# TensorE transposes by 64-row halves, and softmax sums divided out on the rows of x, in a fused attention and mixture-of-experts kernel

## The chip, the cores and the metric

The kernel runs on one core of one Trainium2 chip. The metric is the device time of one execution in microseconds (us). Three runs of the kernel before gave a median of 738.96 us (736.74 to 739.04).

## The reference

The three stages are chained. All arithmetic is float32.

```python
# attention: q, k, v are [4 batches, 8 heads, 576 rows, 64]; a band mask of 64 keys
scores = (1 / sqrt(64)) * q @ k.T                 # kept where 0 <= row - key < 64
attn = exp(scores - max); attn /= attn.sum() + 1e-9
x = (attn @ v) as [2304 rows, 8 heads * 64]
# mixture of experts, top 1 of 8, 512 -> 1024 -> 512
logits = x @ w_gate + modality_bias[modality_id]
e = argmax(logits); gate = softmax(logits)[e]
x = gate * (relu(x @ w1[e]) @ w2[e])
# feed-forward, 512 -> 2048 -> 512
h = x @ w_in
out = (h - tanh(h)) @ w_out
```

## The kernel before, in words

**Attention.** A batch has five groups: four head pairs (`t_pair`) of 512 rows, and one tail (`t_tail`) with the last 64 rows of all heads. `t_prep` turns the k and then the q of a pair with four TensorE transposes of 128x128 each (L611, L619), each into one PSUM bank; DVE copies k out (`t_kcopy`, L638), ACT or DVE copies q out (L628, L630). A pair then has four TensorE bursts: scores of both heads (L709, L722), transposes of the probabilities P in 16 halves of 64 rows that go to two banks (L747), and P times v (L761). Between scores and transposes stands `t_soft`, once per head: DVE takes the row maxima (L790), ACT the exponentials and their sums (L793), DVE adds 1e-9 to the sums and inverts them (L796, L797), and POOL or DVE multiplies P by the result (L799). `t_xout` copies the product to xT, which holds x with the channels on the partitions.

**Routing** (`route`, once per batch). L901 multiplies xT by the gate weights, 32 columns per head pair; `t_logit` copies the partial logits out; L918 turns them and sums over the four head pairs by a product with a 0/1 matrix `sel`. DVE then finds the expert and the gate value, and the place of each row in its expert's list. `t_xrow` turns a tile of 128 rows of x with four full transposes (L873) into one bank, one ACT or DVE instruction multiplies by the gate (L879, L881), and SP sends the tile to DRAM (L884): five tiles a batch, 20 in all.

**Experts.** Five units hold the rows of one expert each: four of 504 rows (four blocks of 126) and one of 288 (126, 126 and 36). Two of them are formed early, from batch 0 and from batches 0 to 2. `t_gather` fetches the rows of a unit from DRAM, `t_xsplit` turns them with full transposes (L1306), one bank for each of four column blocks, and `t_xsplit1` (L1316, L1319) makes a high and a low part. `t_stream` runs the two matrix products (L1381, L1401) as three products of high and low parts. `t_wload` and `t_wsplit` (L392, L394, L1356) bring and split the weights. `t_conv` decodes the 64-bit weights of the feed-forward in the background.

**Feed-forward** (`second`): L1788 and L1836, in six chunks of 384 rows.

**Order of the work.** Everything up to the feed-forward is ordered before the launch by a planner, `Flow`: each task yields operations with an engine (or a choice of engines with a price each), the tasks it waits for, the PSUM banks it may take (`bank`, `nb` of them) and a priority. `Flow.pick` takes the engine that could start first and, of the operations ready on it, the one with the lowest priority number. A pseudo-random `nudge` from one SEED is added to the priorities from 0 to 30 on all engines but SP. The engines then run their queues in that order and wait only on semaphores. Attention may use banks 0 to 3, 6 and 7 (`bankA`), routing and x banks 4 and 5 (`bankX`), the experts' products 6 and 7 (`bankE`).

## Time and profile before

| what | before |
|---|---|
| median of three runs | 738.96 us (736.74 to 739.04) |
| the profiled execution | 737.28 us |
| its span, first to last instruction | 735.5 us |
| TensorE (PE) busy | 721.0 us, 98% of the span |
| VectorE (DVE) busy | 568.8 us, 77% |
| ScalarE (ACT) busy | 509.2 us, 69% |
| GpSimd (POOL) busy | 318.3 us, 43% |
| granted TensorE clock, mean | 0.997 |

Times are from the profile of one execution; 1.8 us of it lie outside the span. Matmuls overlap, and the ends of them are modelled, so a burst of matmuls is read from its first start to the start of the next burst, and not from its busy time. PEld is the load of the stationary operand. "Idle before" is the time in which the engine stood still before an instruction, followed by what ended it.

### The profile page before, as it was taken

The numbers are of one execution on the slowest core, as the hardware profiler recorded it, in microseconds if no ns is written. First come the engines' busy times: TensorE is split into PE (matmuls) and PEld (weight loads), VectorE is DVE, ScalarE is ACT, GpSimd is POOL, SyncE is SP. The second block draws the span as 40 slices with busy tenths as digits, with TensorE's granted clock in tenths as the row PEclk, the third lists the DMA queues.
The fourth block names the chain that finished last, engine by engine and source line by source line (L and its number), as shares of the span: only waits on it lengthen the run. The fifth ranks groups of instructions, "written<-read, shape, count | busy, mean of one in ns | idle before, by whom it ended". The sixth has DMA issues, their size and how long they took to land.

```text
span 735.5 us, 14501 instructions
## 1 busy us (share of the span) xinstructions
PE 721.0 (98%) x4939; PEld 625.3 (85%) x4939; DVE 568.8 (77%) x1104; ACT 509.2 (69%) x1225; POOL 318.3 (43%) x351
## 2 busy tenths in 40 slices
PE   7999999999999999999999999999999999999995
PEld 5888877788888887999998998989989899898994
DVE  5888995979988997739999876767677676757663
ACT  4888985646667665738888776767667666766662
POOL 6786762532524323206784442434234233423222
PEclk9999999999999999999999999999999999999998
DMA  9988937587887875730010110101011000001001
GB/s 202 211 187 192 249 87 217 175 259 208 253 261 238 267 240 183 203 96 1 12 32 1 45 44 0 45 12 33 0 44 29 15 24 21 23 1 44 1 0 48
DMA packets 119249, 77.30 MB, mean 105 GB/s; under 512 B 54968, under 2 KB 112332, under 8 KB 119166
## 3 DMA queue, kind: packets, MB, share of 16 engines
q1 hardware_dynamic: 114822, 66.38, 32.8%
q0 software_dynamic: 3264, 9.63, 4.2%
q8 instruction: 41, 0.67, 0.4%
q10 hardware_dynamic: 1080, 0.28, 0.2%
q14 instruction: 42, 0.34, 0.1%
HBM read 62.10 MB, written 14.16 MB: 104 GB/s over the span
## 4 chain that ended last, share of the span: by engine, by line
PE 88%; DVE 6%; ACT 1%; DMA 1%; issue 1%; POOL 1%; POOLq 0%; SPq 0%; DVEq 0%; ACTq 0%
PE ps_g L1788 27%; PE ps_q L1836 26%; PE bank L1401 14%; PE bank L1381 13%; PE bank L722 1%; PE bank L1306 1%; DVE nm L790 1%; PE bank L761 1%; DMA kr<-in_k 1%; PE bank L747 1%; DMA va<-in_v 1%; ACT P L793 1%; PE bank L873 1%; PE ps_q L1788 1%; PE bank L901 1%
## 5 line engine op out<-in xcount | busy, mean ns | idle before, releaser
L1819 POOL TENSOR_TENSOR gl<-gv,gh 128x384 fp32r<-128x384 f32 x95 | 102.1, 1074 | 169.4 <-ACT gh L1818 167.4
L1806 DVE SCALAR_TENSOR_TENSOR gv<-gu,ps_g 128x384 f32<-128x384 f32 x94 | 51.8, 551 | 84.7 <-ACT gt L1801 84.4
L1836 PE MATMUL ps_q<-H,gl 128*128 128x512 f32 x288 | 114.0, 396 | 0.0
L1818 ACT ACTIVATE gh<-gv 128x384 fp32r<-128x384 f32 x96 | 50.2, 523 | 91.8 <-issue 87.2
L1836 PE MATMUL ps_q<-H,gh 128*128 128x512 f32 x288 | 113.3, 394 | 0.0
L1810 DVE COPY_PREDICATED gv<-gm,gt 128x384 f32<-128x384 int32 x96 | 77.1, 803 | 9.9
L1356 DVE TENSOR_TENSOR wl<-raw,wh 128x512 fp32r<-128x512 f32 x78 | 64.7, 848 | 13.3 <-ACT wh L392 12.5
L1809 DVE SCALAR_TENSOR_TENSOR gv<-gs,gv 128x384 f32<-128x384 f32 x96 | 65.8, 686 | 10.7 <-ACT gt L1801 0.5
L1836 PEld LDWEIGHTS ps_q<-H,gl 128*128 128x128 f32 x288 | 54.1, 188 | 12.9 <-DVE gl L1819 0.3
L1803 ACT ACTIVATE gs<-gu,pa 128x384 f32<-128x384 f32 x96 | 59.0, 614 | 8.0 <-DVE gv L1809 8.0
L1802 ACT ACTIVATE gs<-gu,pa 128x384 f32<-128x384 f32 x96 | 59.2, 616 | 5.6 <-DVE gv L1808 5.6
L1836 PEld LDWEIGHTS ps_q<-H,gh 128*128 128x128 f32 x288 | 54.1, 188 | 9.0 <-ACT gh L1818 0.2
L1808 DVE SCALAR_TENSOR_TENSOR gv<-gs,gv 128x384 f32<-128x384 f32 x96 | 60.4, 629 | 0.0
L1805 ACT ACTIVATE gm<-gu,pth 128x384 f32<-128x384 f32 x96 | 58.5, 610 | 0.0
L1807 DVE TENSOR_TENSOR gt<-ps_g,gt 128x384 f32<-128x384 f32 x94 | 51.7, 550 | 0.0
L1800 ACT ACTIVATE gu<-ps_g 128x384 f32<-128x384 f32 x94 | 44.4, 472 | 1.6 <-PE ps_g L1788 1.6
L1801 ACT ACTIVATE gt<-ps_g 128x384 f32<-128x384 f32 x94 | 45.4, 483 | 0.0
L392 ACT ACTIVATE wh<-raw 128x512 fp32r<-128x512 f32 x72 | 43.5, 626 | 0.0
L392 ACT ACTIVATE ys<-bank 128x504 f32<-128x504 f32 (+1 forms) x20 | 11.1, 556 | 46.7 <-PE bank L1401 30.2
L1381 PE MATMUL bank<-xl,wh 128*128 128x504 f32 (+1 forms) x160 | 41.5, 376 | 0.0
L1381 PE MATMUL bank<-xh,wh 128*128 128x504 f32 (+1 forms) x160 | 41.1, 375 | 0.0
L1381 PE MATMUL bank<-xh,wl 128*128 128x504 f32 (+1 forms) x160 | 40.8, 373 | 0.0
(479 smaller groups left out, 2028.2 us busy)
## 6 DMA issues: line engine op xcount, KB each, us to landing
raw<-in_w SPq DMA_DIRECT2D x80, 256.0 KB, 4.2
craw<-in_win SPq DMA_DIRECT2D x16, 512.0 KB
craw<-in_wout SPq DMA_DIRECT2D x16, 512.0 KB, 5.0
va<-in_v SPq DMA_DIRECT2D x32, 128.0 KB, 4.9
yd<-ys SPq DMA_DIRECT2D x16, 252.0 KB, 2.3
yr<-yd SPq DMA_DIRECT2D x20, 192.0 KB, 3.0
kr<-in_k SPq DMA_DIRECT2D x11, 256.0 KB, 3.5
qr<-in_q SPq DMA_DIRECT2D x10, 256.0 KB, 4.7
```

Of the source, the lines that this page charges most:

```text
L1356: self.eng(r).tensor_tensor(lo, w, hi.bitcast(F32), op=ALU.subtract)
L1381: nc.tensor.matmul(ps, wt[:, k, :], xt[:, k, :n], start=(k == 0 and q == 0), stop=(k == 3 and q == 2))
L1401: nc.tensor.matmul(ps, wt[:, k % 4, :], h, start=(q == 0), stop=(q == 3 * NF1 - 1))
L1788: nc.tensor.matmul(ps, w[:, c, :], x[:, c, :], start=(c == 0 and i == 0), stop=(c == 3 and i == 2))
L1802: nc.scalar.activation(s1, u, AF.Square, bias=self.pa1)
L1803: nc.scalar.activation(s2, u, AF.Square, bias=self.pa2)
L1805: nc.scalar.activation(m, u, AF.Relu, bias=self.pth)
L1808: nc.vector.scalar_tensor_tensor(v, s1, b1, v, op0=ALU.add, op1=ALU.mult)
L1809: nc.vector.scalar_tensor_tensor(v, s2, b2, v, op0=ALU.add, op1=ALU.mult)
L1810: nc.vector.copy_predicated(v, m.bitcast(I32), t)
L1819: (nc.vector if last else nc.gpsimd).tensor_tensor(gl, v, gh.bitcast(F32), op=ALU.subtract)
L1836: self.nc.tensor.matmul(self.po[t], g[:, t * 128 : t * 128 + 128], w, start=(f == 0 and i == 0), stop=(f == NF2 - 1 and i == 2),)
```

## The change

Every TensorE transpose of up to 128 rows is made as two transposes of 64 rows (`halves`); the upper and the lower half go to different banks. This holds for k and q (now one operation for both, with two banks, each with a half of k and a half of q, copied out by four instructions of half the size instead of two), for P of the tail, for the rows of x in `t_xrow`, for the gathered rows in `t_xsplit` (two operations of two column blocks instead of four of one), and for the partial logits in `route`, where the product with `sel` is replaced by transposes. P of the pairs was made so already.

The softmax of the head pairs is no longer divided before the product with v. ACT's sums go to a tile `heads` of the batch, [128, 5 tiles, 8 heads]; `route` adds 1e-9 and inverts it once per batch. The gate weights are put into 16 columns per head, so that the partial logits stand apart by head; DVE multiplies them by the inverted sums and adds the heads. `t_scale` multiplies the inverted sums by the gate, and `t_xput` copies each half of a tile of x out of its bank and multiplies it by them: ACT copies and POOL or DVE multiplies in place, or DVE does both at once. The tail keeps the old order (its part of `heads` is set to 1).

In the planner an operation has a form ("full", "rows", "quads", "cols", "heads"); a change of form on TensorE costs TURN, an operation of the last form has its priority number lowered by STICK, and the seed depends on the batch. Many prices are set anew. `bankX` has banks 0 and 1 too. The high parts of the weights of the first unit may be made by POOL.

In the diff cut to its core, left out are the tail's P, the body of the copies of k and q, the rest of `t_xsplit1` (which now takes a half of two column blocks at a time, one instruction of the same size as before on ACT and on DVE for each), prices alone, and memsets.

```diff
-NUDGE, SEED = 1.0, 78
+NUDGE, SEEDS = 1.0, (17, 17, 88, 60, 17)
+TURN, STICK = 0.095, 1.0
...
-    def nudge(self, n):
-        x = (n + 1) * (2 * SEED + 1) * 2654435761 % 2**32
+    def nudge(self, n, p):
+        x = (n + 1) * (2 * SEEDS[int(p / 5) if 0 <= p < 20 else -1] + 1) * 2654435761 % 2**32
         return NUDGE * ((x ^ x >> 15) * 2246822519 % 2**32 >> 8) / 2**24
...
         def prio(th):
             p = th[0] if th[3].prio is None else th[3].prio
-            return (p + self.nudge(th[1]) if e != "SP" and 0 <= p < 30 else p), th[1]
+            if e == "PE" and 0 <= p < 30 and th[3].form == self.form:
+                p -= STICK
+            return (p + self.nudge(th[1], p) if e != "SP" and -STICK <= p < 30 else p), th[1]
         _, s, th = min((x for x in best[e] if x[0] <= lo), key=lambda x: prio(x[2]))
-        return e, s, th
...
+                if e == "PE":
+                    self.form = op.form
...
-        self.bankA, self.bankX, self.bankE = {0, 1, 2, 3, 6, 7}, {4, 5}, {6, 7}
+        self.bankA, self.bankX, self.bankE = {0, 1, 2, 3, 6, 7}, {4, 5, 0, 1}, {6, 7}
...
+        self.heads = [self.rt.tile([128, RT, 2 * 4], F32, name=f"heads{b}") for b in range(B)]
...
-        nc.vector.tensor_copy(self.wgp[:, :, 0:E], wg)
+        for h in range(2):
+            s = slice(64 * h, 64 * h + 64)
+            nc.vector.tensor_copy(self.wgp[s, :, 16 * h : 16 * h + E], wg[s])
...
+    def halves(self, outs, x, n=128):
+        for h in range((n + 63) // 64):
+            s = slice(64 * h, min(64 * h + 64, n))
+            self.nc.tensor.transpose(outs[h][..., : s.stop - s.start], x[s], self.idF[s, s])
     def t_prep(self):
-        nc, R = self.nc, self.rings
+        R = self.rings
         for pi in range(4 * B):
             b, hp = divmod(pi, 4)
             base = 5 * b + hp - 0.75
-            r = yield Op(("PE", 0.45), [self.tk("qp", "k", pi)], [R["kT"].ask(pi)], bank=self.bankA | self.bankX, prio=base)
+            r = yield Op(
+                ("PE", 0.55), self.tks("qp", [("k", pi), ("q", pi)]), [R["kT"].ask(pi)], bank=self.bankA | self.bankX, prio=base,
+                nb=2, form="rows",
+            )
             self.raw["kTr", pi] = r.rel[0]
             self.raw["T", pi] = r.rel[0].x
...
+            ps = [self.bt(r, 128, 512, i=h).rearrange("p (w c n) -> p w c n", w=2, c=4) for h in range(2)]
+            for w, x in enumerate("kq"):
+                x, rel = self.raw["qp", x, pi]
+                for c in range(4):
+                    self.halves([p[:, w, c] for p in ps], x[:, c].rearrange("p h d -> p (h d)"))
+                for t in rel:
+                    t.t = r.t
...
+            for h in range(2):
+                self.flow.add(self.t_kcopy(pi, h, ps[h], r.tok), base)
+                self.flow.add(self.t_qcopy(pi, h, ps[h], r.tok), base)
+                self.flow.add(self.t_join(self.tks("qkc", [(pi, h, 0), (pi, h, 1)]), [r.bts[h]]), base)
+            for w, x in enumerate(("kT", "qT")):
+                self.flow.add(self.t_join(self.tks("qkc", [(pi, 0, w), (pi, 1, w)]), [self.tk(x, pi)]), base)
+            self.flow.add(self.t_ktail(pi), 1.25 * pi + 0.25)
...
+    def t_qcopy(self, pi, h, ps, tok):
+        r = yield Op(dict(ACT=0.31, DVE=0.34), [tok])
...
+    def t_kcopy(self, pi, h, ps, tok):
+        r = yield Op(dict(DVE=0.34, ACT=0.31), [tok])
...
     def t_soft(self, key, ps, P, bs, tok):
         nc, at = self.nc, self.at
+        g, h = key
+        b, hp = divmod(g, 5)
         r = yield Op(("DVE", 0.6), [tok])
         nm = at.tile([128, 4], F32, name="nm", bufs=8)
-        sm = self.sums[self.nsum % len(self.sums)]
-        self.nsum += 1
-        rc = at.tile([128, 4], F32, name="rc", bufs=8)
         nc.vector.tensor_reduce(nm, ps, op=ALU.max, axis=AX.X, negate=True)
         r = yield Op(("ACT", 1.37), [r.tok])
+        if hp < 4:
+            sm = self.heads[b][:, :, 2 * hp + h : 2 * hp + h + 1]
+        else:
+            sm = self.sums[b % 2][:, :, 0:1]
         for j in range(4):
-            nc.scalar.activation(P[:, j, :], ps[:, j, :], AF.Exp, bias=nm[:, j : j + 1], accum_out=sm[:, j, 0:1])
+            nc.scalar.activation(P[:, j, :], ps[:, j, :], AF.Exp, bias=nm[:, j : j + 1], accum_out=sm[:, j])
         bs.t = r.t
-        r = yield Op(("DVE", 0.3), [r.tok])
-        nc.vector.tensor_reduce(rc, sm, op=ALU.add, axis=AX.X)
-        nc.vector.reciprocal(rc, rc)
-        r = yield Op(dict(POOL=0.98, DVE=0.62), [r.tok], bias=dict(DVE=1.2))
-        self.eng(r).tensor_tensor(P, P, rc[:, :, None].to_broadcast([128, 4, 128]), op=ALU.mult)
+        if hp == 4:
+            r = yield Op(("DVE", 0.3), [r.tok])
+            rc = at.tile([128, 4], F32, name="rc", bufs=2)
+            nc.vector.tensor_reduce(rc, self.sums[b % 2], op=ALU.add, axis=AX.X)
+            nc.vector.reciprocal(rc, rc)
+            r = yield Op(dict(POOL=0.98, DVE=0.62), [r.tok], bias=dict(DVE=1.2))
+            self.eng(r).tensor_tensor(P, P, rc[:, :, None].to_broadcast([128, 4, 128]), op=ALU.mult)
         self.tk("P", *key).t = r.t
...
     def t_xrow(self, t):
-        nc, R = self.nc, self.rings
         m = 128 if i < RT - 1 else 64
-        r = yield Op(("PE", 0.45), [], [R["xr"].ask(t)], bank=self.bankX)
+        o = (b % 2) * S + 128 * i
+        r = yield Op(("PE", 0.275), [], [self.rings["xr"].ask(t)], bank=self.bankA | self.bankX, nb=2, form="rows")
         rel = r.rel[0]
-        ps, bk = self.bt(r, 128, 4, 128)[:m], r.bt
-        o = (b % 2) * S + 128 * i
+        ps = [self.bt(r, 128, 4, 64, i=h)[:m] for h in range(2)]
         for hp in range(4):
-            nc.tensor.transpose(ps[:, hp, :], self.xT[:, hp, o : o + m], self.idF)
+            self.halves([p[:, hp] for p in ps], self.xT[:, hp, o : o + m])
         self.tk("xr", t).t = r.t
-        r = yield Op(dict(ACT=0.52, DVE=0.6), [r.tok])
+        for h in range(2):
+            self.flow.add(self.t_xput(t, h, rel.x[:m], ps[h], r.bts[h], r.tok), -6 + 0.01 * t)
         xr = rel.x[:m]
...
+        yield Op(None, self.tks("xe", [(t, 0), (t, 1)]))
+        r = yield Op(("SP", DQ), wire=1.0, lag=2.6)
+        self.nc.sync.dma_start(self.xs[b * S + 128 * i : b * S + 128 * i + m, :], xr)
         rel.t = r.t
         self.tk("xs", t).t = r.t
+    def t_xput(self, t, h, xr, ps, bk, tok):
+        nc = self.nc
+        b, i = divmod(t, RT)
+        xo = xr.rearrange("p (a h d) -> p h a d", a=4, h=2)[:, h]
+        sc = self.heads[b][: xr.shape[0], i, :].rearrange("p (a h) -> p h a", h=2)[:, h, :, None].to_broadcast(xo.shape)
+        r = yield Op(dict(ACT=0.31, DVE=0.36), [tok, self.tk("scale", b)])
+        if r.e == "ACT":
+            nc.scalar.activation(xo, ps, AF.Copy)
+            bk.t = r.t
+            r = yield Op(dict(POOL=0.54, DVE=0.34), [r.tok], bias=dict(DVE=0.5), lock=True)
+            self.eng(r).tensor_tensor(xo, xo, sc, op=ALU.mult)
+        else:
+            nc.vector.tensor_tensor(xo, ps, sc, op=ALU.mult)
+            bk.t = r.t
+        self.tk("xe", t, h).t = r.t
...
         toks = self.tks("lt", [(b, 0), (b, 1)])
         sh = [128, n, E]
-        r = yield Op(("PE", 0.23 * n), toks, bank=self.bankX)
-        ps, bk = self.bt(r, 128, n, E), r.bt
+        r = yield Op(("DVE", 0.4), self.tks("P", [(5 * b + p, h) for p in range(4) for h in range(2)]), lock=True)
+        hd = self.heads[b]
+        nc.vector.tensor_scalar(hd[:, 0 : n - 1], hd[:, 0 : n - 1], 1e-9, None, op0=ALU.add)
+        nc.vector.reciprocal(hd[:, 0 : n - 1], hd[:, 0 : n - 1])
+        r = yield Op(("PE", 0.075 * n), toks + [r.tok], bank=self.bankX, nb=2, form="rows")
+        ps = [self.bt(r, 128, n, 64, i=k) for k in range(2)]
         for i in range(n):
-            w = 128 * i
-            nc.tensor.matmul(ps[:, i, :], self.ltT[:, w : w + 128], self.sel, start=True, stop=True, skip_group_check=True)
-        r = yield Op(("DVE", 0.6), [r.tok], lock=True)
+            self.halves([p[:, i] for p in ps], self.ltT[:, 128 * i : 128 * i + 128])
+        bks = r.bts
+        r = yield Op(("DVE", 0.7), [r.tok], lock=True)
...
+        for k in range(2):
+            nc.vector.tensor_tensor(
+                lh[:, :, 4 * k : 4 * k + 4],
+                ps[k].rearrange("p n (s w) -> p n s w", w=16)[:, :, :, 0:E],
+                hd[:, :, 4 * k : 4 * k + 4, None].to_broadcast([128, n, 4, E]),
+                op=ALU.mult,
+            )
+        for bk in bks:
+            bk.t = r.t
+        r = yield Op(("DVE", 1.0), lock=True)
+        nc.vector.tensor_reduce(Lg, lh.rearrange("p n s e -> p n e s"), op=ALU.add, axis=AX.X)
+        nc.vector.tensor_tensor(Lg, Lg, self.btok[:, t0:t1, :], op=ALU.add)
         nc.vector.tensor_reduce(mx, Lg, op=ALU.max, axis=AX.X)
         nc.vector.tensor_tensor(Lg, Lg, mx[:, :, None].to_broadcast(sh), op=ALU.subtract)
-        bk.t = r.t
...
+        self.flow.add(self.t_scale(b, r.tok), -7)
...
+    def t_scale(self, b, tok):
+        r = yield Op(dict(POOL=0.3, DVE=0.22), [tok], bias=dict(DVE=0.2), lock=True)
+        hd, g = self.heads[b], self.gate[:, RT * b : RT * b + RT, None]
+        self.eng(r).tensor_tensor(hd, hd, g.to_broadcast([128, RT, 8]), op=ALU.mult)
+        self.tk("scale", b).t = r.t
...
-        for c in range(4):
-            r = yield Op(("PE", 0.11 * len(u.blocks)), [], [R["xh"]] if c == 0 else [], bank=self.bankX)
+        for c in (0, 2):
+            r = yield Op(("PE", 0.14 * len(u.blocks)), [], [R["xh"]] if c == 0 else [], bank=self.bankX, nb=2, form="rows")
...
+            ps = [self.bt(r, 128, 512, i=h).rearrange("p (c j n) -> p c j n", c=2, j=4) for h in range(2)]
+            for k in range(2):
+                d = (c + k) * 128
+                for j, _, m in u.blocks:
+                    self.halves([p[:, k, j] for p in ps], u.xg[:m, j, d : d + 128], m)
+            if c == 2:
                 u.xgr.t = r.t
-            self.flow.add(self.t_xsplit1(i, c, ps, bk, r.tok), -1)
-
...
-        r = yield Op(dict(ACT=0.52, DVE=0.4), [tok], [R["wh"]], lock=True)
+        by = dict(ACT=0.5, DVE=0.4) if i else dict(ACT=0.5, DVE=0.4, POOL=0.6)
+        r = yield Op(by, [tok], [R["wh"]], lock=True, bias=None if i else dict(ACT=0.6, DVE=0.6))
...
-        r = yield Op(by, [r.tok], [R["wl"]], bias=dict(POOL=LATE), lock=True)
+        r = yield Op(by, [r.tok], [R["wl"]], bias=dict(POOL=LATE if i else 0.0), lock=True)
```

## Rows read from the trace of the kernel before

**Rows 1.** Busy time by stage, all engines (--windows): engine busy (count), clock, DMA share, GB/s.

```profile
20.00:94.00 74.00, 72.50 (x1374) 60.32 (x1374) 66.61 (x193) 64.55 (x265) 54.94 (x83) 1.00 0.89 205
94.00:140.00 46.00, 45.27 (x435) 35.66 (x433) 35.32 (x101) 32.06 (x88) 22.73 (x27) 1.00 0.61 178
140.00:325.00 185.00, 184.63 (x911) 155.60 (x912) 156.48 (x272) 112.86 (x209) 61.74 (x48) 1.00 0.73 220
325.00:735.00 410.00, 402.72 (x2019) 363.30 (x2018) 298.72 (x494) 289.02 (x618) 165.48 (x151) 0.99 0.07 23
```

**Rows 2.** Page, part 4: the chain that ended last, by engine.

```profile
PE 88%; DVE 6%; ACT 1%; DMA 1%; issue 1%; POOL 1%; POOLq 0%; SPq 0%; DVEq 0%; ACTq 0%
```

**Rows 3.** Timeline of PE, 19.8 to 25 us: start, duration, instruction, count, idle before.

```profile
19.89 0.71 PE L747 MATMUL bank<-idF,P 64*128 64x64 f32 x16 [0.34 <-POOL P L799]
20.53 0.69 PE L709 MATMUL bank<-mF,idB 64*64 64x512 bf16 x2
...
23.30 0.66 PE L611 MATMUL bank<-idF,craw 128*128 128x128 f32 x4
23.79 0.60 PE L619 MATMUL bank<-idF,qr 128*128 128x128 f32 x4
24.32 0.46 PE L747 MATMUL bank<-idF,cva 64*128 64x64 f32 x8
24.62 0.41 PE L747 MATMUL bank<-idF,cvr 64*128 64x64 f32 x8
```

**Rows 4.** Load of the stationary operand (PEld) by shape, 0 to 325 us: busy, mean ns.

```profile
L747 PEld LDWEIGHTS bank<-idF,P 64*128 64x128 f32 x176 | 6.7, 139 | 3.6 <-issue 1.0 <-POOL P L799 1.0 <-POOL craw L490 0.5
L611 PEld LDWEIGHTS bank<-idF,craw 128*128 128x128 f32 x40 | 4.3, 141 | 0.8 <-issue 0.5
```

**Rows 5.** Timeline of PE, 75 to 79 us: full transposes behind full transposes.

```profile
75.65 0.60 PE L611 MATMUL bank<-idF,kr 128*128 128x128 f32 x4
76.09 0.60 PE L873 MATMUL bank<-idF,xT 128*128 128x128 f32 x4
```

**Rows 6.** Timeline of PE, 105 to 113 us: rows of x within the experts' products.

```profile
107.69 0.66 PE L873 MATMUL bank<-idF,xT 128*128 128x128 f32 x4
108.10 0.70 PE L1381 MATMUL bank<-xh,wl 128*128 128x504 f32 x2
```

**Rows 7.** Timeline of PE, 185 to 187 us: transposes of a unit of 504 rows.

```profile
185.19 1.89 PE L1306 MATMUL bank<-idF,xg 126*128 126x126 f32 x16
186.84 0.70 PE L1401 MATMUL bank<-hh,wh 128*128 128x504 f32 x2
```

**Rows 8.** Timeline of PE, 66 to 68 us: partial logits times `sel`.

```profile
66.56 1.18 PE L918 MATMUL bank<-sel,ltT 128*128 128x8 f32 x10
67.59 0.38 PE L807 MATMUL bank<-mG,idB 128*128 128x512 bf16 x1
```

**Rows 9.** Timeline of PE, 10 to 13 us and 54 us: two waits.

```profile
12.01 1.10 PE L722 MATMUL bank<-kT,qT 64*64 64x128 f32 x32 [1.22 <-DVE qT L630]
...
54.07 1.24 PE L873 MATMUL bank<-idF,xT 128*128 128x128 f32 x8 [0.71 <-ACT xr L879]
```

**Rows 10.** Groups by shape on DVE, ACT and POOL, 0 to 140 us: busy, mean ns.

```profile
L796 DVE TENSOR_REDUCE rc<-sum 128x4 f32<-128x8 f32 x36 | 5.4, 151 | 1.7 <-ACT P L793 1.1 <-ACT cvr L793 0.4
L797 DVE RECIPROCAL rc<-rc 128x4 f32<-128x4 f32 x36 | 6.4, 178 | 1.2
L638 DVE COPY kT<-bank 128x512 f32<-128x512 f32 x13 | 8.8, 679 | 1.1 <-PE bank L611 0.8 <-POOL craw L490 0.3
L683 DVE COPY kTt<-bank 128x256 f32<-128x256 f32 x4 | 1.6, 408 | 0.0
...
L392 ACT ACTIVATE xT<-bank 128x256 f32<-128x256 f32 x2 | 0.8, 385 | 1.9 <-PE bank L837 1.8
...
L799 POOL TENSOR_TENSOR P<-P,rc 128x512 f32<-128x512 f32 x25 | 26.9, 1077 | 13.3 <-DVE rc L797 6.6 <-ACT PT L392 2.3 <-ACT P L793 1.5
```

**Rows 11.** Busy time of the stretch in which DVE and ACT together did most.

```profile
80.00:90.00 10.00, 9.68 (x170) 8.21 (x162) 9.72 (x25) 9.46 (x41) 6.58 (x10) 1.00 0.95 268
```

More of the change, by code (lines that the diff above doesn't have):

```diff
@@ L165, in __init__ @@
         self.wire, self.th, self.n, self.floor = 0.0, [], 0, 0.0
+        self.form = "full"
         self.hold = dict(DVE=(0.0, 0.0), POOL=(0.0, 0.0))
@@ L437, in front @@
         nc.vector.memset(self.qbt, 0.0)
+        for t in self.heads:
+            nc.gpsimd.memset(t[:, RT - 1, :], 1.0)
         for t in self.sums:
@@ L656, in t_preptail @@
         last = [self.tk("S", 5 * b - 1)] if b else []
-        r = yield Op(("PE", 0.45), [self.tk("tl", b)], bank=self.bankA | self.bankX, prio=base)
+        r = yield Op(("PE", 0.25), [self.tk("tl", b)], bank=self.bankA | self.bankX, prio=base, form="rows")
         tl, rel = self.raw["t", b]
@@ L666, in t_preptail @@
         self.flow.add(self.t_ktcopy(b, pk, bk, tk), base)
-        r = yield Op(("PE", 0.4), bank=self.bankA | self.bankX, prio=base)
+        r = yield Op(("PE", 0.2), bank=self.bankA | self.bankX, prio=base, form="rows")
         pq, bq, tq = self.bt(r, 128, 4, 128), r.bt, r.tok
@@ L703, in t_pair @@
         q, k = self.raw["T", pi]
[L704 removed]
+        r = yield Op(("PE", 1.12), [], [R["P"].ask(g, 2)], bank=self.bankA, nb=2, form="quads")
         ps = [self.bt(r, 128, 4, 128, i=h) for h in range(2)]
@@ L739, in t_pair @@
         self.tk("T", g).t = max(t.t for t in tp)
-        r = yield Op(("PE", 0.64), tp, [R["PT"], R["PT"]], bank=self.bankA, nb=2)
+        r = yield Op(("PE", 0.55), tp, [R["PT"], R["PT"]], bank=self.bankA, nb=2, form="rows")
         pt = [self.bt(r, 128, 512, i=c).rearrange("p (h s q) -> p h s q", h=2, s=4) for c in range(2)]
@@ L754, in t_pair @@
         yield Op(None, tp + self.tks("va", [pi]) + self.tks("vb", [pi]))
-        r = yield Op(("PE", 1.08), bank=self.bankA)
+        r = yield Op(("PE", 0.985), bank=self.bankA, form="cols")
         po = self.bt(r, 128, 8, 64)
@@ L820, in t_tail @@
         self.tk("T", g).t = tp.t
-        r = yield Op(("PE", 0.45), [tp], [R["PT"]], bank=self.bankA)
-        pt = self.bt(r, 128, 4, 128)
+        r = yield Op(("PE", 0.275), [tp], [R["PT"]], bank=self.bankA, nb=2, form="rows")
+        pt = [self.bt(r, 128, 4, 64, i=h) for h in range(2)]
         PT = at.tile([128, 2, 4, 64], F32, name="PT", bufs=NPT).rearrange("p a b c -> p (a b c)")
@@ L825, in t_tail @@
         for j in range(4):
-            nc.tensor.transpose(pt[:, j, :], P[:, j, :], self.idF)
+            self.halves([p[:, j] for p in pt], P[:, j])
         rel.t = r.t
         rel = r.rel[0]
-        self.flow.add(self.t_ptcopy((g, 0), PT, pt, r.bt, r.tok), g)
-        yield Op(None, [self.tk("PT", g, 0), self.tk("vt", b)])
-        r = yield Op(("PE", 0.5), bank=self.bankA)
+        for h in range(2):
+            self.flow.add(self.t_ptcopy((g, h), PT[:, :, 64 * h : 64 * h + 64], pt[h], r.bts[h], r.tok, 0.55), g)
+        yield Op(None, self.tks("PT", [(g, 0), (g, 1)]) + [self.tk("vt", b)])
+        r = yield Op(("PE", 0.52), bank=self.bankA, form="cols")
         po = self.bt(r, 128, 4, 64)
@@ L897, in route @@
         for hf in range(2):
-            r = yield Op(("PE", 0.5), self.tks("O", range(5 * b, 5 * b + 5)), bank=self.bankX)
+            r = yield Op(("PE", 0.49), self.tks("O", range(5 * b, 5 * b + 5)), bank=self.bankX, form="heads")
             ps = self.bt(r, 128, 288)
@@ new lines, in t_xsplit @@
+            for k in range(2):
[3 more added lines that the diff above has]
+            if c == 2:
+                u.xgr.t = r.t
+            for h in range(2):
+                self.flow.add(self.t_xsplit1(i, c, h, ps[h], r.bts[h], r.tok), -1)
+            for x in ("xh", "xl"):
+                ends = self.tks(x, [(i, c), (i, c + 1)])
+                self.flow.add(self.t_join(self.tks(x + "p", [(i, c, 0), (i, c, 1)]), ends), -1)
@@ new lines, in t_xsplit1, with at, src @@
+    def t_xsplit1(self, i, c, h, ps, bk, tok):
+        nc, u = self.nc, self.us[i]
+        m = u.blocks[-1][2]
+        full = len(u.blocks) - (m < BR)
+        parts = [(slice(0, full), min(64, BR - 64 * h))]
+        if full < len(u.blocks) and m > 64 * h:
+            parts.append((slice(full, full + 1), min(64, m - 64 * h)))
+        s = sum((p.stop - p.start) * 2 * n for p, n in parts) / 504
+        def at(x, p, n):
+            a = p.start * BR + 64 * h
+            if p.stop - p.start == 1:
+                return x[:, c : c + 2, a : a + n]
+            return x[:, c : c + 2, p.start * BR : p.stop * BR].rearrange("p c (j r) -> p c j r", r=BR)[:, :, :, 64 * h : 64 * h + n]
+        def src(p, n):
+            return ps[:, :, p.start, :n] if p.stop - p.start == 1 else ps[:, :, p, :n]
+        r = yield Op(("ACT", 0.37 * s + 0.13 * len(parts)), [tok])
+        for p, n in parts:
+            nc.scalar.activation(at(u.xh, p, n), src(p, n), AF.Copy)
+        self.tk("xhp", i, c, h).t = r.t
+        r = yield Op(("DVE", 0.53 * s + 0.08 * len(parts)), [r.tok])
+        for p, n in parts:
+            nc.vector.tensor_tensor(at(u.xl, p, n), src(p, n), at(u.xh, p, n).bitcast(F32), op=ALU.subtract)
+        self.tk("xlp", i, c, h).t = r.t
```

96 lines of the change are left out of this document (29 added, 67 removed).

## The prediction, made before the change was run

> **What bounds the kernel now.** I read the busy time by stage first [rows 1]. From 20 us on PE is never idle for long: 72.5 of 74 us up to 94, 45.3 of 46 up to 140, 184.6 of 185 up to 325, 402.7 of 410 after it. From 94 us on the experts' products fill every hole that attention leaves, and the feed-forward, which the change does not touch, begins when they end. The chain of waits says the same: 88% of the span is PE [rows 2]. So work taken off PE is time, as long as something else does not take its place. What could is in the same row: from 20 to 94 us DVE is busy 66.6 and ACT 64.6 of 74 us, POOL 54.9, the DMA engines 89%. After 140 us ACT has 72 us to spare.
>
> Busy time hides what a matmul costs, so bursts are read from start to start. Four full transposes cost 0.49 us for k (23.30 to 23.79) and 0.53 for q (23.79 to 24.32) [rows 3]; in front of other full transposes, 0.44 (75.65 to 76.09) [rows 5]. The difference of 0.09 is the price of a change of form. Eight blocks in 16 halves, the form that P of the pairs already has, cost 0.64 us (19.89 to 20.53), and four blocks of these 0.30, or 0.075 a block (24.32 to 24.62) [rows 3]. A full block costs 0.11 (0.44 / 4).
>
> One thing speaks against halves: the load of a half takes 139 ns and that of a full block 141 [rows 4]. It is not cheaper; two halves must overlap, and 0.075 us for both says that they do. The Trainium skill (TensorE: Matmul & The Clock Gate, section "LDWEIGHTS (loading the stationary operand)") says that a load's time follows the columns alone, however few rows are loaded. By that alone a half would cost what a block costs. It is weighed as a rival below.
>
> **The change, part by part: PE.**
> - k and q: 16 pairs, 0.49 + 0.53 = 1.02 against 0.64 for the same eight blocks: 0.38 x 16 = 6.1 us.
> - Rows of x: four blocks in halves are 0.64 - 4 x 0.075 = 0.34. Before they took 0.44 [rows 5], and 0.41 within the experts' products (107.69 to 108.10) [rows 6]. Half of the 20 tiles lie on either side of 94 us: 10 x 0.10 + 10 x 0.07 = 1.7.
> - Gathered rows: 16 blocks took 1.65 (185.19 to 186.84) [rows 7], and in halves 0.64 + 8 x 0.075 = 1.24: 0.41 for each of four units and some 0.3 for the smaller one: 1.9.
> - Partial logits: ten matmuls took 1.03 (66.56 to 67.59) [rows 8]; five blocks in halves are 0.64 - 3 x 0.075 = 0.42: 0.6 x 4 = 2.5.
> - P of the tail: 0.49 to 0.34, four times: 0.6.
>
> That is 12.8 us. Full transposes stand among the experts' products without a change of form; halves do not. Some 20 groups there (10 tiles of x, eight of gathered rows, two of logits) pay one change that 0.34 does not hold yet: 20 x 0.09 = 1.8. The planner now joins groups of one form. At most each of the 16 groups of k and q saves one change, 1.4; at least none. I take the middle, 0.7. PE is left with 12.8 - 1.8 + 0.7 = 11.7 us less.
>
> **DVE, ACT and POOL.** Off DVE go the sum and the inverse of 32 heads: 32 x (151 + 178) ns = 10.5 us [rows 10]. Copies in two halves cost more: 2 x 408 - 679 = 137 ns on DVE (a half takes 385 ns on ACT, about the same) for each of 32 copies of k and q, 20 of x and four of the tail: 7.7 us, on DVE or ACT. Routing gains two products of 160 elements (at most 408 ns each), a sum over 320 (between 408 and 679) and three small steps (178): 1.3 to 1.9 us, so 1.6 x 4 = 6.4. In all 3.6 us more on both together. From 20 to 94 us lie 12 of the pairs and three quarters of the heads, but only 10 tiles of x and two routings: -7.9 + 3.3 + 1.4 + 0.4 + 3.2 = +0.4.
>
> POOL loses up to 32 multiplications of 1077 ns [rows 10] and gets 40 of half the size, some 0.54 us each: it is relieved by about 13 us. If DVE makes the 40 instead, that is 40 x 0.41 = 16 us more there. The high parts of the first unit's weights may move to POOL, a relief that I leave uncounted.
>
> **What the stage can give.** The same counts put 12 x 0.38 + 10 x 0.10 + 2 x 0.6 + 3 x 0.15 + 0.4 = 7.6 us of PE's gain between 20 and 94 us. But DVE and ACT need 66.6 + 64.6 + 0.4 = 131.6 us there. The fullest ten microseconds hold 9.72 + 9.46 = 19.2 of 20 [rows 11]. At that rate the stage cannot be shorter than 131.6 / 1.92 = 68.6 us, a gain of 5.4 and not 7.6. So 2.2 us are given back. PE's queue then stands in front of scores and P transposes, waiting for ACT's exponentials. If these engines kept up fully, nothing is given back.
>
> **Waits.** Before 20 us the chain from scores to P loses the inverse and the multiplication, and the copies of k and q go to two engines at once; PE waited 1.22 us there for one copy [rows 9]. I take 1.0 us (0 to 2). There the loads follow one another closely, so not more. The tiles of x reach DRAM later, by a multiplication of 0.54 and a small scaling. Behind them stand SP's queue, the gathers and the first unit; PE has attention left when that unit starts at 94 us, so I cost it at nothing. Without that cover it would be half a microsecond for each of two early units. The new sum in routing, 1.6 us, sits in the same chain under the same cover. Decoding of the feed-forward weights stays behind the experts' 185 us, in which ACT is busy 113 [rows 1].
>
> **Sum.** 11.7 - 2.2 + 1.0 = 10.5 us. From the profiled execution, 737.28 us (span 735.5), that is 726.8; the median of the runs, 738.96, lies 1.7 above that execution, and from it the sum gives 728.5. I forecast 728.
>
> **Rivals.**
> 1. DVE and ACT are the bound already, so attention up to 94 us does not get shorter at all: PE's gain of 7.6 us there becomes waiting, and 11.7 - 7.6 = 4.1 us remain: 735 from the median, 732 to 737. For it: 90% and 87% of busy time in that stage [rows 1], and the 16 us if DVE makes the multiplications. Against it: stretches with 96% [rows 11], and a shorter chain per head.
> 2. Slower: PE waits for the second bank. Groups that took one bank now need two at once, and a bank of k and q is held until both of its copies are done. PE waited 0.71 us for a bank in front of the rows of x [rows 9]. Some 44 groups are exposed (16 of k and q, 20 of x, four of logits, four tails). From 15 such waits on, 15 x 0.71 = 10.6, the gain is gone; if every second group waits, 22 x 0.71 = 15.6, the time is 744. For it: eight banks for all. Against it: k and q already held two, x may now use all eight, and the copies are half as long.
> 3. The change does not do what it says: halves in the new places run one behind the other, a pair at 0.11 like a full block. Then only turns and copies are left, 739 to 741. If each half cost a whole block, 0.22 a pair, nearly 300 blocks would add 33 us: 770. This is the page's rule on loads taken alone. The 0.075 of [rows 3] is the same instruction with the same loads, so 4 in 100 for both, and 1 of these for the second.
>
> **How the numbers follow.** The forecast's case has 0.60, with a range of its own from 722 (nothing given back, all joins, 2 us of waits) to 732; rival 1 has 0.25, rival 2 0.09, rival 3 0.04, and 0.02 are for a new order of the queue that costs PE a little. A measurement can tell about 0.3% from no change, 2.2 us: under 736.7 is faster, over 741.2 slower. Faster: 0.60 and most of rival 1, 0.83. The same: the rest of rival 1 and most of rival 3, 0.08. Slower: 0.09. The range of 8 in 10 goes from 721.5 to 736, which takes in most of rival 1 and leaves out rivals 2 and 3.
>
> **What would show it.** In the changed profile: 16 halves of k and q from start to start in about 0.64 us and four blocks of x in about 0.34; the first feed-forward matmul near 315 us instead of 325, and nothing new after it; PE's idle time from 20 to 94 us up by some 2 us, put down to ACT or DVE; POOL under 54.9 us there. Rival 1 would show the first experts' product still near 94 us and new waits of PE for P or for the copies of k and q; rival 2, waits in front of transposes, put down to copies out of a bank; rival 3, pairs of halves at 0.11. The prediction is wrong if the feed-forward starts before 308 or after 322 us.

## The result, and the profile after

20 runs of the changed kernel gave a median of 743.25 us (736.19 to 748.46) against 737.03 us for 20 runs of the kernel before, taken beside them: ratio 1.0063, 95% interval 1.0039 to 1.0087. The ratio is one of means and leaves out the two slowest runs of the changed kernel, which count as slow; the two medians alone would give 1.0084. The changed kernel is slower by 0.6%, and outside the forecast's range. The kernel before was run again beside each set of experiments (medians of 737.0 to 738.8 us), so runs of different sets are compared by their ratios. The profiled execution took 739.21 us (span 737.4), 4 us less than its median, so its trace shows less of the loss than the runs do.

The page's busy times and its chain of waits by engine:

```profile
PE 712.3 (97%) x5235; PEld 617.1 (84%) x5235; DVE 573.3 (78%) x1084; ACT 508.8 (69%) x1255; POOL 306.3 (42%) x359
PE 74%; DVE 12%; issue 4%; DMA 3%; ACT 2%; POOL 2%; SPq 2%; POOLq 0%; DVEq 0%; ACTq 0%
```

PE has lost 8.7 us of busy time, and the chain runs through PE for 74% of the span instead of 88% [rows 2].

The prices of the halves came out as forecast. PE's timeline (start, duration, instruction, count): k and q of a pair, a unit's gathered rows, partial logits.

```profile
65.61 0.41 PE L618 MATMUL bank<-idF,kr 64*128 64x64 f32 x8
65.87 0.41 PE L618 MATMUL bank<-idF,qr 64*128 64x64 f32 x8
66.12 0.22 PE L683 MATMUL bank<-idF,tl 64*128 64x64 f32 x1
...
120.66 0.52 PE L618 MATMUL bank<-idF,ltT 64*128 64x64 f32 x10
121.11 1.19 PE L1465 MATMUL bank<-xh,wl 128*128 128x504 f32 x4
...
188.34 1.21 PE L618 MATMUL bank<-idF,xg 64*128 64x64 f32 x32
189.49 0.73 PE L1485 MATMUL bank<-hh,wh 128*128 128x504 f32 x2
```

From start to start 0.51 us for k and q among other halves (0.64 forecast, a change of form included), 0.45 for the logits (0.42) and 1.15 for the gathered rows (1.24; 1.65 before [rows 7]). Now the stages of [rows 1], with the same columns:

```profile
20.00:94.00 74.00, 67.05 (x1512) 56.24 (x1511) 62.38 (x178) 64.52 (x287) 39.07 (x71) 0.93 0.89 195
94.00:140.00 46.00, 42.84 (x466) 33.04 (x461) 39.72 (x99) 30.13 (x85) 30.50 (x44) 0.96 0.63 181
140.00:325.00 185.00, 183.38 (x953) 153.82 (x954) 154.89 (x277) 112.65 (x212) 62.04 (x51) 0.99 0.73 224
```

Two things are new. PE stands idle: 7.0 us up to 94 us (1.5 before) and 3.2 up to 140 (0.7). And its clock, which before was granted in full for as long as PE had work, is at 0.93, 0.96 and 0.99 on average, the lower of its two levels (1.2 GHz) for a time, which costs about 74 x 0.07 + 46 x 0.04 + 185 x 0.01 = 9 us. So the work that PE was spared, 11.7 us by the forecast's count, has become waits and a slower PE. The first feed-forward matmul, before and after:

```profile
325.22 0.34 PE L1788 MATMUL ps_g<-yh,win0H 128*128 128x384 f32 x1
...
326.33 0.34 PE L1872 MATMUL ps_g<-yh,win0H 128*128 128x384 f32 x1
```

It starts 1.1 us later than before, not 10 earlier.

### The profile page after: what moved, and what is told of

It reads as the page before. It is cut to its first block, busy times and chain, and to the rows that moved or that the text cites. A ratio compares the mean times of both kernels' runs of the same rounds, so it can differ in the third digit from the quotient of the medians.

```text
span 737.4 us, 15072 instructions
## 1 busy us (share of the span) xinstructions
PE 712.3 (97%) x5235; PEld 617.1 (84%) x5235; DVE 573.3 (78%) x1084; ACT 508.8 (69%) x1255; POOL 306.3 (42%) x359
## 4 chain that ended last, share of the span: by engine, by line
PE 74%; DVE 12%; issue 4%; DMA 3%; ACT 2%; POOL 2%; SPq 2%; POOLq 0%; DVEq 0%; ACTq 0%
PE ps_q L1920 21%; PE ps_g L1872 21%; PE bank L1485 14%; PE bank L1465 12%; DVE gv L1893 2%; DVE gv L1892 2%; DMA va<-in_v 2%; PE bank L783 1%; PE bank L618 1%; DMA kr<-in_k 1%; DVE nm L811 1%; SPq L530 1%; PE bank L769 1%; DVE gv L1890 1%; ACT gs L1887 1%
## 5 line engine op out<-in xcount | busy, mean ns | idle before, releaser
L1893 DVE SCALAR_TENSOR_TENSOR gv<-gs,gv 128x384 f32<-128x384 f32 x96 | 68.0, 708 | 10.0
L1440 DVE TENSOR_TENSOR wl<-raw,wh 128x512 fp32r<-128x512 f32 x77 | 59.8, 795 | 9.1 <-ACT wh L397 8.7
L1892 DVE SCALAR_TENSOR_TENSOR gv<-gs,gv 128x384 f32<-128x384 f32 x96 | 64.0, 666 | 0.0
L397 ACT ACTIVATE wh<-raw 128x512 fp32r<-128x512 f32 x69 | 41.7, 624 | 0.0
```

Of the source, the lines that this page charges most:

```text
L1440: self.eng(r).tensor_tensor(lo, w, hi.bitcast(F32), op=ALU.subtract)
L1892: nc.vector.scalar_tensor_tensor(v, s1, b1, v, op0=ALU.add, op1=ALU.mult)
L1893: nc.vector.scalar_tensor_tensor(v, s2, b2, v, op0=ALU.add, op1=ALU.mult)
```

## Experiments

### Is it the granted clock? Is it the first unit's place in the queue?

`fill_most` and `fill_half` put products of ones (bf16, 128x128 by 512 columns, their result overwritten) where the plan has PE wait, so that PE is quiet less often. `x_banks` frees the first unit's transposes from waiting for banks 4, 5, 0 and 1: its first product stood at 94.0 us before and at 103.5 after.

```diff
 # fill_most (45 products in all; fill_half has int(gap * 0.5 / 0.22), 24 products)
+            if e == "PE" and self.free[e] > 9.0:
+                gap = s - self.free[e]
+                r.fill = max(0, int((gap - 0.15) / 0.22))
...
 # x_banks, t_xsplit
-bank=self.bankX, nb=2, form="rows"
+bank=self.bankX if i else self.bankA | self.bankX, nb=2, form="rows"
```

> The changed kernel, with 45 products of a 128x128 tile of ones with 512 columns put on TensorE in front of operations before which the plan lets it wait (as many as the planned wait less 0.15 us holds); their result is overwritten. Clock theory: the granted clock fell to 1.2 GHz in four stretches of 17.1 us because TensorE had waited, and that cost 8.5 us; with the waits filled it stays at 2.4 GHz up to the end, the feed-forward starts at 317 to 320 us instead of 326 and the time is 729 to 734 us. Order theory: TensorE lacks work since the first unit starts 9.5 us later, and the clock only goes along; the fillers leave 740 to 746 us, or add up to 10 us.

> The same with 24 such products, for half of each planned wait. Clock theory: fewer or shorter stretches at 1.2 GHz than the 17.1 us of the changed kernel, time between 729 and 740 us. Order theory: 740 to 746 us, whatever the clock does.

> The changed kernel, with the transposes of the first unit's gathered rows allowed in all eight PSUM banks instead of four. Order theory (they waited for two of four banks: rows landed at 82.4 us, transposes at 93.1): transposes 4 to 8 us earlier, the first expert product at 95 to 99 us instead of 103.5, and the time 4 to 8 us less, 735 to 739. Clock theory: the time goes with the microseconds at 1.2 GHz, whatever the start of the unit: half of these microseconds more or less than 8.5 us, from 735 to 747.

Measured: 740.4 us (1.0033, 1.0012 to 1.0054), 741.5 (1.0046, 1.0016 to 1.0076) and 741.2 (1.0024, 1.0005 to 1.0043). With 45 products the clock of the profiled run is 0.995 instead of 0.985, yet the first unit's product still stands at 103.5 us and the feed-forward at 328.1. The higher clock has not brought the work forward: what PE waits for there is late anyway. With more banks that product comes 5.9 us earlier (97.6), but the feed-forward comes at 329.4: an earlier first unit does not bring the end forward. All three ratios stand a little under the changed kernel's 1.0063, with intervals that overlap its own.

### Is it DVE's load, the softmax, the draw of the order?

Two kernels leave out the row maximum (24.5 us of DVE), `soft_back` divides P in its place again and keeps the multiplications of the rows of x and of the logits, by ones, and `after_s11` changes the seeds alone.

```diff
 # after_nomax (before_nomax alike); their seeds are 3 and 0
-        nc.vector.tensor_reduce(nm, ps, op=ALU.max, axis=AX.X, negate=True)
-            nc.scalar.activation(P[:, j, :], ps[:, j, :], AF.Exp, bias=nm[:, j : j + 1], accum_out=sm[:, j])
+            nc.scalar.activation(P[:, j, :], ps[:, j, :], AF.Exp, accum_out=sm[:, j])
 # soft_back, t_soft
-        if hp == 4:
+        if True:
...
 # after_s11
-NUDGE, SEEDS = 1.0, (17, 17, 88, 60, 17)
+NUDGE, SEEDS = 1.0, (11, 11, 11, 11, 11)
```

> The kernel before with the row maximum of the softmax left out (the exponential gets no bias; 36 reductions of 0.68 us, 24.5 us of DVE's work between 9 and 108 us, are gone), and the plan drawn anew with seed 0. Pace theory (DVE and ACT limit what TensorE can do in attention only once TensorE has been made faster): here TensorE is still the bound, it had 4.8 us of idle time between 8 and 142 us, so 733 to 737 us, a gain of 1 to 4. Order theory (the fixed order of the queues decides, not the load of an engine): within 2 us of before, either side.

> The changed kernel with the row maximum left out in the same way (24.5 us less on DVE), seed 3 in every batch. Pace theory: TensorE's saved 12 us come to light once DVE has room, so 730 to 735 us, 8 to 12 below the changed kernel, and at least 4 below the kernel before without its maxima; the granted clock stays at 2.4 GHz through attention. Order theory: 739 to 744 us, like the changed kernel, and not below the kernel before without its maxima.

> The changed kernel with the softmax divided in its place again (36 sums and reciprocals of 0.15 and 0.18 us on DVE, 36 multiplications of P on POOL or DVE are back; the rows of x and the logits are multiplied by ones, so that work stays), seed 16 in every batch. Pace theory: 11 us of DVE's work and about 8 us of multiplications that DVE takes over come on top of a stage that DVE and ACT limit, so 746 to 756 us. Order theory: within 3 us of the changed kernel. If dividing on the rows of x is itself what cost time, 735 to 739 us.

> The changed kernel with the seeds of its plan alone changed, 11 in every batch. Pace theory: 739 to 744 us, as the changed kernel, whatever the order. Order theory: outside 739 to 744 us on one side or the other, since the order of the first unit's steps is drawn anew.

Measured: 733.5 us (0.9945, 0.9929 to 0.9962), 739.5 (1.0023, 1.0005 to 1.0041), 748.1 (1.0144, 1.0123 to 1.0166) and 740.1 (1.0049, 1.0032 to 1.0066). The pace theory falls in the form it had: freed DVE gives the changed kernel 0.4%, no more than the kernel before (0.55%). The divisions of P, put back, cost 0.8% (6 us); since the multiplications on the rows of x stay in that kernel, this is the price of work on top, and does not show whether the rows of x are the better place to divide. Another order stands at 1.0049, within the changed kernel's interval, and is still slower than before.

### Is it the loads?

Four kernels don't load q (k's rows are used in its place); two of them leave out the maximum as well. Each has a seed of its own.

```diff
 # after_noq, load_qk and t_prep (before_noq, before_both, after_both alike)
-        for t, src in ((k, "k"), (q, "q")):
+        for t, src in ((k, "k"),):
-                x, rel = self.raw["qp", x, pi]
+                x, rel = self.raw["qp", "k", pi][0], self.raw["qp", x, pi][1]
```

> The kernel before without q's loads (k's rows are transposed in their place, so 4.2 MB less are read until about 80 us), seed 29. Load theory (the 16 DMA engines, busy at a share of about 1.0 up to 50 us, are what the changed kernel ran into): here TensorE is the bound, 733 to 737 us. Joint theory (loads, DVE with ACT, and the last batch's routing each stand a few us behind TensorE): 733 to 736 us. Order theory: within 2 us of before.

> The changed kernel without q's loads in the same way, seed 78 in every batch. Load theory: 728 to 734 us, and the waits for loads before 40 us are gone. Joint theory: 736 to 740 us, a gain of 2 to 5, for DVE and ACT hold the pace next, as the run without the maxima gained 3.7 alone. Order theory: 740 to 744 us.

> The kernel before without q's loads and without the row maximum, seed 4. All theories: TensorE is the bound throughout, 312.4 us of work ahead of the feed-forward less what the last idle 3 us give: 731 to 734 us, no better by more than 2 than without the maxima alone (733.5).

> The changed kernel without q's loads and without the row maximum, seed 16 in every batch. Joint theory: with both covers away TensorE's saved work shows at last, 722 to 730 us, at least 4 below the kernel before with the same two left out, and TensorE idle for under 8 us ahead of the feed-forward (13.5 in the changed kernel). Load theory: the same time as without q's loads alone, within 3. Order theory: 738 us or more.

The whole times (2408 to 2422 us) say nothing: other scores route the rows otherwise, and work follows after the feed-forward's start that the other kernels don't have. Up to the feed-forward the work is the same, and I read its start instead, in one profile each: 324.3, 328.9, 318.6 and 318.8 us (325.2 before, 326.3 after). Loads alone are not it. With both covers gone the changed kernel's attention does get ahead, its last scores stand at 87.7 us instead of 106.2, and yet the feed-forward starts no earlier than in the kernel before treated alike. Something behind attention takes it back. `after_both`, DVE's and PE's timelines (in brackets the idle time before and who ended it):

```profile
131.92 0.27 DVE L1205 TENSOR_REDUCE eu<-le 1x16 f32<-1x128 f32 x1
132.23 0.19 DVE L1206 TENSOR_SCALAR eu<-eu 1x16 f32<-1x16 f32 x1
132.46 4.74 DVE L1208 TENSOR_SCALAR em<-eu 1x16 f32<-1x16 f32 x1
137.23 0.28 DVE L1210 TENSOR_TENSOR ou<-iom,em 1x128 f32<-1x128 f32 x1
...
139.15 0.29 PE L1065 MATMUL bank<-rhs,ob 128*126 128x160 bf16 x1 [5.98 <-DVE xl L1399]
```

An operation on 16 numbers takes 4.74 us and ends at 137.20 us; on POOL one product follows the other until 137.17. That operation belongs to the table of units that DVE makes after the last batch's routing.

### The table after the last batch

The same place in the changed kernel, DVE, then POOL, then PE:

```profile
137.74 0.26 DVE L1208 TENSOR_REDUCE eu<-le 1x16 f32<-1x128 f32 x1
138.04 2.71 DVE L1209 TENSOR_SCALAR eu<-eu 1x16 f32<-1x16 f32 x1
140.78 0.16 DVE L1211 TENSOR_SCALAR em<-eu 1x16 f32<-1x16 f32 x1
...
141.26 0.30 DVE L1076 TENSOR_TENSOR T<-T,bank 126x160 f32<-126x160 f32 x1
...
132.39 1.23 POOL L1063 TENSOR_TENSOR ob<-ob,tbase 128x630 bf16<-128x630 bf16 x1
133.59 1.19 POOL L921 TENSOR_TENSOR xr<-xr,heads 128x256 f32<-128x256 f32 x2
134.74 1.19 POOL L921 TENSOR_TENSOR wout2W<-wout2W,heads 128x256 f32<-128x256 f32 x2
135.88 1.19 POOL L921 TENSOR_TENSOR wout0W<-wout0W,heads 128x256 f32<-128x256 f32 x2
137.04 1.23 POOL L921 TENSOR_TENSOR wout1W<-wout1W,heads 64x256 f32<-64x256 f32 x2
138.24 2.48 POOL L1440 TENSOR_TENSOR wl<-raw,wh 128x512 fp32r<-128x512 f32 x2
...
138.00 0.77 PE L618 MATMUL bank<-idF,xg 64*128 64x64 f32 x17
141.62 0.81 PE L618 MATMUL bank<-idF,xg 62*128 62x62 f32 x15 [2.85 <-DVE T L1076]
```

POOL works without a break from 128.5 to 140.7 us: the last batch's ten multiplications of rows of x, and the split of the first unit's weights pushed behind them. DVE's operation of 0.16 us ends at 140.75 us, when POOL's run ends (140.72). PE waits 2.85 us for a bank that DVE empties behind it (into T, from which the addresses of the gathers are made), and at 142.1 us, half a microsecond after that wait, PE's clock falls to 1.2 GHz for 3.4 us (0.83 on average in the ten microseconds from 140):

```profile
140.00:150.00 10.00, 8.38 (x42) 6.87 (x43) 9.04 (x36) 3.24 (x6) 2.61 (x4) 0.83 0.39 113
```

Before, the same operation took 0.16 us, POOL was silent from 138.7 to 143.6, and PE waited 0.8 us:

```profile
139.33 0.16 DVE L1148 TENSOR_SCALAR eu<-eu 1x16 f32<-1x16 f32 x1
...
140.37 0.65 PE L1306 MATMUL bank<-idF,xg 126*128 126x126 f32 x4 [0.83 <-DVE T L1021]
```

`x_act` lets ACT scale the last batch's rows as it takes them out of their banks (28 calls; three of the ten halves fell to DVE). `x_act_s11` has the seeds of `after_s11`. `x_quiet` keeps the late weight splits off POOL too. `before_xpool` gives the kernel before POOL's ten multiplications, by ones.

```diff
 # x_act, t_xput
+        late = b == B - 1
+        r = yield Op(dict(ACT=0.95 if late else 0.31, DVE=0.36), [tok, self.tk("scale", b)])
+        if r.e == "ACT" and late:
+            for a in range(4):
+                g = self.heads[b][: xr.shape[0], i, 2 * a + h : 2 * a + h + 1]
+                nc.scalar.activation(xo[:, a], ps[:, a], AF.Copy, scale=g)
...
 # before_xpool, t_xrow
+        if b == B - 1:
+            for h in range(2):
...
+                nc.gpsimd.tensor_tensor(xo, xo, sc, op=ALU.mult)
```

> The changed kernel, its seeds kept; the last batch's ten halves of rows of x are scaled as ACT takes them out of their banks (four calls of 64 columns each) and no longer multiplied on POOL, ten operations of 0.60 us between 128 and 138 us. Contention theory (in the changed kernel the table after the last batch, a chain of short DVE operations, is held up while POOL works without a break: 10.2 us from 131.05 to 141.26 us against 7.1 before, one operation of 0.2 us lasting 2.7 beside a product on POOL): the chain takes 7 to 8 us again, TensorE's wait of 2.9 us and the 3.4 us at 1.2 GHz behind it go, 738 to 741 us. Joint theory (attention itself is late, by loads and DVE): 742 to 744 us, as the changed kernel.

> The same with seed 11 in every batch, in whose plan TensorE waited 6.2 us for the table (16 us from the chain's first operation to its last, one of 0.08 us lasting 4.8 beside POOL) and ran 6.8 us at 1.2 GHz behind it; 740.1 us. Contention theory: both go, 732 to 736 us, and the feed-forward starts by 322 us (327.2 with the multiplications on POOL). Joint theory: the wait is moved, not removed: 738 to 741 us.

> As the first, and POOL takes no part of the splitting of the first unit's weights from its tenth step on (DVE does those, 0.67 us each), so that POOL is silent while the table is made. Contention theory: the table's chain takes 7 us or less, but DVE has 5 to 7 us more of its own to do between 120 and 140 us, so 738 to 742 us. Joint theory: 743 to 746 us.

> The kernel before, in which POOL multiplies the last batch's rows of x by ones, ten operations of 256 columns, as the changed kernel has them. Contention theory: the table's chain (7.1 us there) takes 9 to 12, TensorE waits 2 to 5 us more at about 140 us, and the time is 740 to 743 us. Joint theory: TensorE has other work to do there, within 1.5 us of before.

Measured: 733.8 us (0.9956, 0.9933 to 0.9979), 733.9 (0.9964, 0.9940 to 0.9988), 735.0 (0.9975, 0.9952 to 0.9998) and, the counter-test, 741.8 (1.0048, 1.0035 to 1.0061). `x_act` is faster than both kernels. Its gain on the changed kernel is 9.5 us between the medians of two sets of runs and 7.9 us by the ratios. The edit redraws the order as well, so one pair alone would not show it; but with two other orders the gain is 6.3 us (seed 11) and 6.0 (seed 3 without the maximum, below). The two single profiles differ by 5.0 us, which is about what the contention theory had counted (738 to 741 us); the rest of the gain lies in runs without a trace. `x_quiet` is no better than `x_act`. The feed-forward of `x_act` starts at 323.0 us, with the other seeds at 322.3 (327.2). `before_xpool` on DVE, POOL and PE:

```profile
142.07 1.19 DVE L1172 TENSOR_SCALAR tab<-tr 1x16 int32<-1x16 f32 x1
143.18 0.30 DVE L1029 TENSOR_TENSOR T<-T,bank 126x160 f32<-126x160 f32 x1
...
140.63 1.30 POOL L890 TENSOR_TENSOR wout2W<-wout2W,one 64x256 f32<-64x256 f32 x2
141.90 2.49 POOL L1364 TENSOR_TENSOR wl<-raw,wh 128x512 fp32r<-128x512 f32 x2
...
143.53 0.65 PE L1314 MATMUL bank<-idF,xg 126*128 126x126 f32 x4 [2.84 <-DVE T L1029]
```

The wait of 2.84 us is now in the kernel before (0.83), with none of the halves. A part of it is order: four operations of the table stand ahead of T's copy here that follow it in the kernel before. They took 0.9 us there and take 2.6 here, two of them 0.81 and 1.19 instead of 0.16. In `x_act` PE has no gap there; busy time from 105 to 150 us, first of the changed kernel, then of `x_act`:

```profile
105.00:150.00 45.00, 42.15 (x360) 32.20 (x359) 38.69 (x102) 24.50 (x69) 28.64 (x38) 0.96 0.60 174
```

```profile
105.00:150.00 45.00, 45.00 (x384) 34.32 (x384) 38.09 (x107) 25.60 (x84) 27.87 (x35) 1.00 0.65 189
```

From the start of the table's first operation (`le`, on `upto` and `nB`) to the end of T's copy, with POOL's busy time within it:

| kernel | table, us | POOL busy in it, us |
|---|---|---|
| x_quiet | 5.3 | 2.2 |
| before | 7.4 | 5.2 |
| x_act | 7.8 | 6.0 |
| before_xpool | 10.1 | 10.1 |
| after | 10.5 | 9.7 |
| x_act_s11 | 10.7 | 7.1 |
| after_nomax | 11.7 | 9.7 |
| after_both | 15.8 | 11.5 |
| after_s11 | 16.4 | 12.6 |

By and large the table takes longer the longer POOL works in it (the expectations took its end a little earlier, 10.2 and 7.1). The table by itself proves little, for a longer one has more room for POOL's work, and in four kernels (`before_xpool`, `x_act_s11`, `after_both`, `after_s11`) more operations stand ahead of T's copy. What shows the hold-up is the single operations of 0.16 us that end when POOL's run ends. What PE loses by it depends on what stands in its own queue: the table of `x_act_s11` takes as long as that of the changed kernel, and PE does not wait there. The Trainium skill (SBUF — State Buffer, section "Who interferes with whom") says that DVE and GpSimd share one pair of ports, which one instruction holds alone, and that casts, tensor-scalar operations and those with two inputs in SBUF can be shut out by it, but not reductions. The trace agrees: the stretched operations are of the first kinds, and the reduction at 137.74 us beside POOL's product takes its 0.26. In length the trace shows more than one instruction: the operation at 138.04 us waited out two products of 1.24 us each.

### What is left

```diff
 # x_actall_s59: late for all batches, seed 59; x_act_fill: x_act with the products of ones;
 # x_act_nomax: after_nomax with x_act's edit
-        late = b == B - 1
+        late = True
```

> The changed kernel without the row maximum, seed 3 as in the run without it, and the last batch's rows of x scaled on ACT instead of multiplied on POOL. In the run without the maximum TensorE waited 5.3 us at 138.8 us and ran 6.8 us at 1.2 GHz behind it, while POOL worked without a break. If the table's hold-up hid what the freed DVE gave: 728 to 733 us, 6 to 11 below 739.5, and at least 3 below the changed kernel with ACT's scaling alone (733.8). If DVE's load never mattered: 733 to 735 us.

> The changed kernel, its seeds kept, with the last batch's rows scaled on ACT, and the idle products of ones put into the waits that the plan shows for TensorE (as in the first runs; their results are overwritten). If the rest of the loss, 6.8 us at 1.2 GHz before 102 us, is the clock's own price: 728 to 731 us and a narrow spread of the runs. If the clock only falls where TensorE would have waited anyway, as in the first runs: 731 to 735 us, narrower than the 731.1 to 741.1 without the products.

> The changed kernel with the rows of x of all four batches scaled on ACT, seed 59 in every batch. If POOL's multiplications hold up the first three batches' routing as they did the last one's, the idle time between 20 and 105 us (9.9 us with the last batch alone on ACT) falls under 7 and the time is 728 to 732 us; if they hid there, ACT, busy for 8 to 9 of each 10 us before 100 us, gets about 20 us more to do and the time is 736 to 742 us.

Measured: 733.4 us (0.9941, 0.9927 to 0.9955), 736.7 (1.0000, 0.9973 to 1.0026) and 737.2 (1.0000, 0.9986 to 1.0014). The table had hidden 6.0 us of the run without the maximum (1.0023), but then DVE's freed time gives nothing beyond `x_act`, and the kernel before without the maximum is as fast (0.9945). Idle products raise the clock of the profiled run from 0.987 to 0.995 and do not shorten the time, so a clock raised in this way gives nothing back. (The 6.8 us of the second expectation are what the low clock costs `x_act` before 102 us; it lasts for 13.6.) Scaling on ACT in every batch is no better than before: PE's idle time from 20 to 105 us is 9.5 us, against 10.0 in `x_act`, and not under 7.

## Why the prediction was wrong

- **PE's terms held.** Bursts measured 0.51, 0.45 and 1.15 us against 0.64, 0.42 and 1.24, and two tiles of x 0.64, or 0.32 for four blocks (127.48 to 128.12; 0.34 forecast); rival 3 is out, for a pair of halves took 0.064 to 0.09 us in these bursts and not 0.11. In the term of the logits, 0.6 x 4 is 2.4 and not 2.5, which changes nothing.
- **The step that failed** is under "Waits": "The tiles of x reach DRAM later, by a multiplication of 0.54 and a small scaling ... so I cost it at nothing", with a half microsecond for each of two early units as its price without cover. I asked who waits for the tiles. No wait of PE in the changed kernel's trace is for them. What costs is who works beside them: ten POOL products and the weight splits behind them, in one run, while DVE makes the last batch's table, behind which PE's next bank is emptied. I counted POOL by its load, "relieved by about 13 us", and it is relieved (39.1 instead of 54.9 us up to 94), but not there: 30.5 instead of 22.7 us from 94 to 140 us [rows 1]. Measured price: 6 to 8 us by the ratios of three pairs of runs, and 3.5 us (0.48%) put on the kernel before. It is why the kernel became slower and not a little faster, and it is about half of the miss: a gain of 10.5 us was forecast, a loss of 4.6 measured.
- **The give-back of 2.2 us up to 94 us was too small.** Of 7.6 us forecast there, PE's idle time took 5.5 (1.5 to 7.0), and the low clock about 5 more, which no step foresaw. The size is that of rival 1: with the table's hold-up taken out, `x_act` gains 3.2 us on the kernel before (0.44%), against 4.1 there and 10.5 in the forecast. Of rival 1's signs, though, one is there and one is not: PE waits for P (1.8 us in four places from 8 to 105 us), but the first experts' product comes at 103.5 us and not near 94. In the same stretch 2.7 us of PE's waits are for loads (packed rows that POOL copies among them) and 3.7 behind DVE's copies out of banks. So the cause is not shown. Less work on DVE alone left PE's idle time from 8 to 105 us at 12.4 us, fewer loads alone at 10.8 (10.6 in the changed kernel); with both left out it fell to 5.3 (one draw of the order each). Loads and DVE may each stand close behind PE; which of the waits goes first is open, and the run without both but with ACT's scaling wasn't tried.
- **Rival 2**, the slower one, named another wait (0.71 us for a second bank, 15 times or more). Waits in front of transposes that end with a copy out of a bank are there, but few: one of 2.85 us, since DVE that empties the bank was held up, and four of 0.5 to 0.8 us before 102 us.
- The feed-forward start at 326.3 us lies outside the 308 to 322 that the forecast named as its own test. So does that of `x_act`, 323.0.

## What to carry to other kernels

When work moves to POOL, look at what DVE does in the same microseconds, not at POOL's total: a chain of short DVE operations beside an unbroken run of POOL products can last until the run ends. A busy share of 98% on the first engine says that its work is time now, not that it still will be when 4% of it is gone; the second wait is found by asking which queue empties the bank or fills the buffer that it needs next. A relief that gives nothing in one run may only be hidden by another wait behind it.
